# Block 0 of a fused WKV and feed-forward kernel: weight words made by two VectorE operations, low bits by ScalarE, gate transposes a slice later

## The chip, the cores and the metric

The kernel runs on one core of a Trainium2 chip. The metric is the device time of one execution in microseconds (us). The engines of the core are TensorE (PE in the rows, its weight loads PEld), VectorE (DVE), ScalarE (ACT), GpSimd (POOL) and SyncE (SP), which issues most of the transfers. Each engine works through its own list of instructions in order; semaphores tie the lists together.

## The reference

Three stages work on 3072 tokens (4 sequences of 768) of 384 channels. The gated feed-forward stage has a hidden width of 1536, and its weights reach the kernel as float64 words; the third stage sends each token to the one of 8 experts with the largest logit.

```
for t in range(S):                                   # attention, per batch and head of 48
    y[:, :, t] = einsum(r_t, state + u * k_t v_t)
    state = w * state + k_t v_t
g = x @ w_gate                                       # feed-forward, 384 -> 1536 -> 384
x = (silu(g) * (x @ w_val)) @ w_out
logits = x @ w_gate2                                 # routing, 8 experts
e = argmax(logits); gate_w = softmax(logits)[e]; eom = sigmoid(x @ w_output_gate)[e]
out = gate_w * eom * (max(x @ w1[e], 0) @ w2[e])
```

## The kernel before

The tokens go in 8 blocks of three tiles of 128 tokens. For each block the feed-forward stage (`b_block`) runs over 12 groups f of 128 hidden columns, and between its steps stand the attention of the block's successor, in pieces, and other small work. The order is written out by hand: each block has a list `slots` of 24 entries, and step f of `b_block` issues, in this order, the g product (`b_up`, nine matmuls into bank 3 or 4), `slots[2f]`, the down product of group f-2 (`b_down`), the v product, the activation (`b_act`: silu on ScalarE, product s on VectorE, the cast h on ScalarE and its rest on GpSimd or, after block 0, on VectorE) and `slots[2f+1]`. This text calls that a step.

Matmuls take each operand as a rounded part (hi) and a rest (lo), three products for one. So each weight group W{f} has a hi and a lo half, and in block 0 they have to be made. For each f a load on SP's queue brings 128 x 2304 int32 words to a tile `raw` (the float64 words, low and high half in turn). `conv_steps` makes float32 bits of them in a tile `cv`: in three chunks of 384 words, three VectorE operations for each (lines 214 to 216), with bank 5 between them. This text calls the whole conv(f). `conv_b` casts cv to the hi half (ScalarE, line 232) and subtracts for the lo half (GpSimd, line 233). `gate_a` turns the third chunk of cv with three TensorE transposes (line 241) into bank 7 and copies it out as `gt` (ScalarE, line 243); `gate_b` multiplies `gt` by the small matrix G (line 249), and three small copies put the result in the last 16 columns of W{f} (lines 252 to 254). The group f can be used by `b_up` once W{f} is there, and by `b_down` once `gate_b` is through.

Bank 7 is shared: by `gate_a` and `gate_b`, by the attention's scores (`a_scores`, line 363, every second matmul) and by its state product (line 427). So whoever writes it waits until the one before has been read.

Before block 0 the program prepares tables and the attention of the first three tiles, and conv(0) and conv(1) are done. In block 0 conv(f) stands behind the activation of step f-3, `conv_b(f)` behind that of step f-2. The attention tiles 3, 4 and 5 stand in slots 0 to 22 (`a_place`: scale, diagonal, scores, output, state). In blocks 2 to 5 `scan_units` loads the weights a second time, squares them on GpSimd (line 265) and takes a minimum on VectorE (line 268); `find_flag` looks at the results near the end.

Of the kernel before, what the change touches and what calls it, by code (L numbers as in the profile page):

```python
# [8 lines left out]
F32 = mybir.dt.float32  # L9
F32R = mybir.dt.float32r  # L10
BF16 = mybir.dt.bfloat16
I32 = mybir.dt.int32
U32 = mybir.dt.uint32
I64 = mybir.dt.int64
AF = mybir.ActivationFunctionType
ALU = mybir.AluOpType
AX = mybir.AxisListType
# [34 lines left out]
def kernel(  # L52
# [30 lines left out]
    tid = cst.tile([P, NT], I32, name="tid")  # L83
    cnt = cst.tile([P, 8], F32, name="cnt")
    pw = cst.tile([P, 2, 4, 8], F32, name="pw")
    bad = cst.tile([P, 2 + NF], F32, name="bad")
    badb = cst.tile([P, 1], BF16, name="badb")
    flag = cst.tile([P, 1], I32, name="flag")
    wT = cst.tile([P, 4], F32, name="wT")
# [28 lines left out]
    def setup_consts():  # L118
        dve.memset(wT, 1.0)
        dve.memset(rev, 0.0)  # L120
        act.activation(out=rev, in_=rev, func=AF.Silu)
        dve.memset(kr3[0], 0.0)
        pool.memset(kr3[1], 0.0)
        for j in range(2):
            sp.dma_start(
                out=wT[64 * j : 64 * j + HD, :],
                in_=w_d.rearrange("(p j) d -> j d p", j=2)[j],
            )
        sp.dma_start(out=ub, in_=u_d.rearrange("h d -> (h d)").partition_broadcast(P))
        make_identity(nc, ident)  # L130
        pool.memset(triu, 1.0)
        pool.affine_select(
            out=triu, in_=triu, compare_op=ALU.is_gt, fill=0.0, base=0,
            pattern=[[1, P]], channel_multiplier=-1,
        )
# [63 lines left out]

    cvs = {}  # L200

    def conv_steps(f):
        raw = raws.pop(f)
        r32 = raw.rearrange("p (n two) -> p n two", two=2)
        lo, hi = r32[:, :, 0], r32[:, :, 1]
        if f % 2 == 0:
            t = cpool.tile([P, FW], I32, tag="rows", name="cv", bufs=1)
        else:
            t = apool.tile([P, FW], I32, tag="cv", name="cv", bufs=1)
        cvs[f] = t.bitcast(F32)  # L210
        p = bank[5][:, 0:DM].bitcast(I32)

        def part(o):
            dve.tensor_scalar(p, hi[:, o], 3, 0x3FFFFFF8, ALU.logical_shift_left, ALU.bitwise_and)  # L214
            dve.scalar_tensor_tensor(p, hi[:, o], -0x40000000, p, ALU.bitwise_and, ALU.bitwise_or)  # L215
            dve.scalar_tensor_tensor(t[:, o], lo[:, o], 29, p, ALU.logical_shift_right, ALU.bitwise_or)  # L216

        return [lambda c=c: part(slice(c * DM, (c + 1) * DM)) for c in range(3)]

    def conv_a(f):  # L220
        for u in conv_steps(f):
# [34 lines left out]
    def scan_units(f):  # L256
        st = {}

        def u0():
            st["raw"] = load_w(f)  # L260

        def u1():
            st["t"] = apool.tile([P, FW], F32, tag="cv", name="sc", bufs=1)
            h = st["raw"].bitcast(F32).rearrange("p (n two) -> p n two", two=2)[:, :, 1]
            pool.tensor_tensor(out=st["t"], in0=h, in1=h, op=ALU.mult)

        def u2():
            dve.tensor_reduce(out=bad[:, 2 + f : 3 + f], in_=st["t"], op=ALU.min, axis=AX.X)

        return [u0, u1, u2]  # L270

    def find_flag():
        few = cpool.tile([P, 1], F32, tag="few", name="few", bufs=1)
        dve.tensor_reduce(out=few, in_=cnt, op=ALU.max, axis=AX.X)
        dve.tensor_scalar(bad[:, 1:2], few, float(CAP), None, ALU.is_gt)
        dve.tensor_scalar(few, few, float(CAPS[0]), None, ALU.is_gt)
        dve.tensor_scalar(bad[:, 2:], bad[:, 2:], TINY * TINY, None, ALU.is_lt)
        dve.tensor_reduce(out=badb, in_=bad, op=ALU.max, axis=AX.X)
        return few

# [332 lines left out]
    def a_place(slots, i, first):  # L613
        e = 1 if i % BT == BT - 1 else 0
        if i + 1 < NT:
            slots[first].append(lambda: a_load(i + 1))
        if i < 2 * BT:
            slots[first + (i == BT)].append(lambda: a_scale(i))
            slots[first + 1].append(lambda: a_diag(i, BT < i))
            slots[first + 3 - e] += [lambda: a_keys(i), lambda: a_scores(i), lambda: a_mask(i)]  # L620
            slots[first + 5 - e] += [lambda: a_out(i), lambda: a_load_kr(i + 1), lambda: a_bonus(i + 1)]
            slots[first + 6].append(lambda: a_state_up(i, 7))
            return
        e = 0
        if i == 2 * BT:
            slots[first] += [lambda: a_scale(i), lambda: a_diag(i, False)]
            slots[first + 2] += [lambda: a_scores(i), lambda: a_next(i), lambda: a_load_kr(i + 1)]
        slots[first + 3 - e].append(lambda: a_keys(i))
        if i + 1 < NT:
            slots[first + 3 - e].append(lambda: a_bonus(i + 1))  # L630
            slots[first + 4 - e].append(lambda: a_scale(i + 1))
        slots[first + 5 - e].append(lambda: a_burst(i))
        if i + 1 < NT:
            slots[first + 5 - e].append(lambda: a_diag(i + 1, False))
            slots[first + 6 - e].append(lambda: a_next(i + 1))
        if i + 2 < NT:
            slots[first + 6 - e].append(lambda: a_load_kr(i + 2))
# [165 lines left out]
    with tc.manual_schedule():  # L803
# [49 lines left out]
        a_load_kr(3)  # L853
        next_w(3)
        next_w(4)
        conv_a(1)
        next_w(5)
        a_bonus(3)
# [2 lines left out]
        for blk in range(NBLK):  # L861
# [6 lines left out]
                for t in range(BT):  # L868
                    a_place(slots, (blk + 1) * BT + t, 8 * t)
            if blk == 0:  # L870
                slots[0][0:0] = [lambda: gate_b(0), lambda: conv_b(1, (GV, OUT)), lambda: gate_a(1), lambda: conv_a(2), lambda: a_state(0, 0)]
                slots[1][0:0] = [lambda: gate_b(1), lambda: conv_b(2), lambda: a_state(1, 1)]
                slots[2][0:0] = [lambda: gate_a(2), lambda: a_state(2, 2), lambda: gate_b(2)]
                for f in range(3, NF):
                    slots[2 * f - 5] += [lambda f=f: conv_a(f), lambda f=f: next_w(f + 2) if f > 3 else None]
                    slots[2 * f - 3].insert(0, lambda f=f: conv_b(f)); slots[2 * f - 3 + (f == 3)].insert(0, lambda f=f: gate_a(f))
                    slots[2 * f - 2].insert(0, lambda f=f: gate_b(f)) if f > 3 else slots[4].append(lambda: gate_b(3))
                slots[19].append(lambda: zts.append(late_consts()))
            else:
                for o, u in zip((4, 7, 7) if blk == NBLK - 1 else (12, 15, 15), c_units(blk - 1)):  # L880
                    slots[o].append(u)
# [286 lines left out]
```

## Time and profile before

| | |
|---|---|
| runs | 859.89, 862.46, 864.29 us; median 862.46 |
| the profiled execution | 861.56 us, of which 859.8 us from the first instruction to the last |
| mean granted TensorE clock | 0.985 |
| busy, share of the span | PE 821.9 us (96%), PEld 792.9, DVE 459.8 (53%), ACT 271.2 (32%), POOL 267.9 (31%) |
| chain that ended last, by engine | PE 84%, DVE 8%, DMA 2%, issue 2%, ACT 1% |
| block 0, roughly 34 to 125 us | the lines 214, 215 and 216 make 2% each of that chain |

TensorE is busy nearly throughout, so the time is moved by what makes it wait, by what it has to do, and by its clock. VectorE is the busiest engine only in the first seventh of the span, where it makes the weight words. The granted clock was half (0.50) in three stretches near 21, 42 to 55 and 117 to 123 us of the span and full nearly everywhere else.

### The profile page before, as it was taken

What the parts mean: (1) busy time and instruction counts of PE and PEld (TensorE: products, weight loads), DVE (VectorE), ACT (ScalarE), POOL (GpSimd) and SP (SyncE); (2) the same over time, 40 slices, a digit from 0 to 9 for tenths busy, and PEclk for the clock granted to TensorE, in tenths of its full rate; (3) what the DMA queues carried; (4) which work ended last, traced back from release to release, by engine and by line L of the source; (5) the groups of instructions that cost most, each with busy time, mean ns of one, the idle gap of its engine ahead of it and who ended that gap; (6) DMA issues with size and microseconds to landing.
All of it is one profiled execution on the core that took longest, in us unless ns stands there. A gap on an engine that the chain in (4) does not pass through costs nothing.

```text
span 859.8 us, 13873 instructions
## 1 busy us (share of the span) xinstructions
PE 821.9 (96%) x5427; PEld 792.9 (92%) x5427; DVE 459.8 (53%) x945; ACT 271.2 (32%) x590; POOL 267.9 (31%) x241
## 2 busy tenths in 40 slices
PE   2888889999999999999999999999999999999996
PEld 2677789999999999999999999999999999999996
DVE  7898753354465456456455434243565565465541
ACT  2434342221222212212212221223454454444432
POOL 6756546223425335245244112010110210121022
PEclk9879989999999999999999999999999999999999
DMA  8615413853322323333323210410394444444201
GB/s 249 247 59 209 146 67 100 249 141 123 105 94 78 129 78 107 109 102 130 116 102 130 60 47 29 161 51 1 118 368 142 167 142 127 158 133 163 85 26 36
DMA packets 29769, 104.90 MB, mean 122 GB/s; under 512 B 5175, under 2 KB 14193, under 8 KB 26624
## 3 DMA queue, kind: packets, MB, share of 16 engines
q1 hardware_dynamic: 26368, 94.37, 34.0%
q0 software_dynamic: 3328, 9.56, 2.9%
q8 instruction: 45, 0.74, 0.4%
q14 instruction: 28, 0.23, 0.1%
HBM read 85.84 MB, written 16.41 MB: 119 GB/s over the span
## 4 chain that ended last, share of the span: by engine, by line
PE 84%; DVE 8%; DMA 2%; issue 2%; ACT 1%; SPq 1%; POOL 0%; POOLq 0%; DVEq 0%; ACTq 0%
PE bank L494 31%; PE bank L513 17%; PE bank L708 12%; PE bank L725 12%; PE bank L363 3%; PE bank L390 2%; PE bank L376 2%; DVE bank L215 2%; DVE bank L214 2%; DMA spare<-in_rkv_dram 2%; DVE cv L216 2%; PE bank L673 1%; PE bank L739 1%; SPq L415 1%; DVE krT L316 1%
## 5 line engine op out<-in xcount | busy, mean ns | idle before, releaser
L494 PE MATMUL bank<-xT,W 128*128 128x384 f32 x1728 | 331.4, 342 | 1.5 <-DMA xT<-stage 1.3
L494 PEld LDWEIGHTS bank<-xT,W 128*128 128x128 f32 x1728 | 305.1, 189 | 5.8 <-DMA xT<-stage 2.2
L513 PE MATMUL bank<-W,h 128*128 128x400 f32 x864 | 176.0, 348 | 0.0
L513 PEld LDWEIGHTS bank<-W,h 128*128 128x128 f32 x864 | 155.9, 189 | 0.5 <-issue 0.2
L505 ACT CAST h<-s 128x384 fp32r<-128x384 f32 x96 | 49.2, 513 | 328.4 <-DVE s L503 328.4
L503 DVE TENSOR_TENSOR s<-s,bank 128x384 f32<-128x384 f32 x96 | 53.2, 554 | 161.4 <-PE bank L494 148.6
L725 PE MATMUL bank<-hd,wf 128*128 128x416 f32 (+1 forms) x576 | 113.9, 344 | 0.0
L725 PEld LDWEIGHTS bank<-hd,wf 128*128 128x128 f32 x576 | 104.3, 188 | 0.7 <-DVE hd L712 0.2
L747 POOL DMA_INDIRECT out_dram<-yo,ix x32 | 35.0, 1095 | 200.6 <-DVE yo L743 174.0
L343 POOL TENSOR_TENSOR at<-ident,a 128x1024 f32<-128x1024 f32 x19 | 36.1, 1897 | 149.2 <-PE bank L494 118.2
L712 DVE SCALAR_TENSOR_TENSOR hd<-bank,hd 128x416 fp32r<-128x416 f32 (+1 forms) x64 | 36.7, 573 | 77.1 <-ACT hd L711 77.1
L506 DVE TENSOR_TENSOR h<-s,h 128x384 fp32r<-128x384 f32 x84 | 51.8, 616 | 48.7 <-ACT h L505 48.7
L657 DVE TENSOR_TENSOR wf<-raw,wf 128x768 fp32r<-128x768 f32 x64 | 61.1, 955 | 7.0 <-ACT wf L656 1.2
L502 ACT ACTIVATE s<-bank 128x384 f32<-128x384 f32 x96 | 47.2, 492 | 47.4 <-PE bank L494 47.4
L575 POOL DMA_INDIRECT xs<-rows,slot x24 | 23.8, 991 | 112.8 <-DVE slot L573 51.5
L711 ACT ACTIVATE hd<-bank 128x416 fp32r<-128x416 f32 (+1 forms) x64 | 32.3, 505 | 82.3 <-PE bank L708 81.9
L708 PE MATMUL bank<-xd1h,wf 128*128 128x416 f32 x192 | 58.2, 361 | 0.0
L656 ACT CAST wf<-raw 128x768 fp32r<-128x768 f32 x64 | 52.8, 825 | 0.0
L368 DVE COPY_PREDICATED at<-mask,bank 128x512 f32<-128x512 int32 x42 | 28.5, 732 | 38.7 <-POOL at L343 35.3
L708 PE MATMUL bank<-xd0h,wf 128*128 128x416 f32 x144 | 43.8, 362 | 0.0
L708 PEld LDWEIGHTS bank<-xd1h,wf 128*128 128x128 f32 x192 | 36.0, 188 | 0.5
L324 POOL TENSOR_TENSOR rkv<-rkv,ub 128x384 f32<-128x384 f32 x21 | 21.8, 1037 | 46.3 <-DMA rkv<-in_rkv_dram 46.3
(175 smaller groups left out, 946.9 us busy)
## 6 DMA issues: line engine op xcount, KB each, us to landing
raw<-in_w_dram SPq DMA_DIRECT2D x36, 768.0 KB, 4.4
raw<-in_w_dram SPq DMA_DIRECT2D x22, 1152.0 KB, 7.1
rkv<-in_rkv_dram SPq DMA_DIRECT2D x21, 576.0 KB, 5.4
krT<-in_krT_dram SPq DMA_DIRECT2D x42, 192.0 KB, 3.4
xs<-zt SPq DMA_DIRECT2D x32, 197.0 KB, 6.0
xr<-xs SPq DMA_DIRECT2D x6, 591.0 KB, 5.7
spare<-in_w_dram SPq DMA_DIRECT2D x2, 1152.0 KB, 9.4
xT<-stage SPq DMA_DIRECT2D x42, 48.0 KB, 2.1
```

The source lines that it names most:

```text
L343: pool.tensor_tensor(out=af, in0=bc(ident, 1, [P, NH, P]), in1=bc(a, 2, [P, NH, P]), op=ALU.mult)
L494: pe.matmul(ps[i], W[f][:, wl, o : o + P], x[:, xl, c, :], start=(c == 0 and n == 0), stop=(c == KC - 1 and n == 2),)
L502: act.activation(out=s, in_=g, func=AF.Silu)
L503: dve.tensor_tensor(out=s, in0=s, in1=v, op=ALU.mult)
L505: act.copy(out=h[:, 0], in_=s)
L506: (pool if blk == 0 else dve).tensor_tensor(out=h[:, 1], in0=s, in1=h[:, 0].bitcast(F32), op=ALU.subtract)
L513: pe.matmul(bank[t][:, 0 : DM + 16], h[:, hl, t * P : (t + 1) * P], W[f][:, wl, 2 * KC * P :], start=(f == 0 and n == 0), stop=(f == NF - ...
L656: act.copy(out=wf[:, 0], in_=raw[:, f])
L657: dve.tensor_tensor(out=wf[:, 1], in0=raw[:, f], in1=wf[:, 0].bitcast(F32), op=ALU.subtract)
L708: pe.matmul(ps, wf[:, wl, c * P : (c + 1) * P], xd[xl][:, c, 0:n], start=(i == 0), stop=(i == 3 * KC - 1))
L712: dve.scalar_tensor_tensor(h[:, 1, 0:n], ps, 0.0, h[:, 0, 0:n].bitcast(F32), ALU.max, ALU.subtract)
L725: pe.matmul(bank[c][:, 0:n], wf[:, wl, o : o + P], h[:, hl, 0:n], start=(f == 0 and i == 0), stop=(f == NEF - 1 and i == 2),)
```

## The change

The word is made of two operations for each chunk in place of three. The first (line 229 of the changed kernel) takes the high word from SBUF, shifts it by three and joins it with a value `n`, also from SBUF, into bank 5. The second (line 230) joins the high word with 0x3FFFFFFF and keeps those bits of the first. `n` holds the three low bits and is made for all 1152 words of a group by one ScalarE operation (`conv_low`, line 214 of the changed kernel), which reads every eighth byte of the raw words. It lies in a spare tile, or in the place where another weight group will be.

The order of block 0 changes with it. `gate_a(f)` stands in `slots[2f-1]` and `gate_b(f)` in `slots[2f]` for every f; before they stood two slots earlier for most f. `conv_low(f)` stands in `slots[2f-6]`, and ahead of the block for f=0 and 1. The consts that `late_consts` makes move from slot 19 to 22, and the state update of a block's third tile in the first two blocks moves two slots ahead. The weight scan takes a maximum beside the minimum, which adds one VectorE reduction of 128x1152 for each of its 12 groups.

```diff
+    def conv_low(f):
+        b3 = raws[f].bitcast(U8).rearrange("p (n e) -> p n e", e=8)[:, :, 3]
+        t = spare[f] if f in spare else wpool.tile([P, 2 * FG], F32, tag=f"W{f}", name=f"low{f}")
+        lows[f] = t[:, 0:FW].bitcast(I32)
+        act.activation(out=lows[f], in_=b3, func=AF.Identity, bias=nb, scale=1.0 / 32)
...
-        def part(o):
-            dve.tensor_scalar(p, hi[:, o], 3, 0x3FFFFFF8, ALU.logical_shift_left, ALU.bitwise_and)
-            dve.scalar_tensor_tensor(p, hi[:, o], -0x40000000, p, ALU.bitwise_and, ALU.bitwise_or)
-            dve.scalar_tensor_tensor(t[:, o], lo[:, o], 29, p, ALU.logical_shift_right, ALU.bitwise_or)
+        def word(o):
+            dve.scalar_tensor_tensor(p, hi[:, o], 3, n[:, o], ALU.logical_shift_left, ALU.bitwise_or)
+            dve.scalar_tensor_tensor(t[:, o], hi[:, o], 0x3FFFFFFF, p, ALU.bitwise_or, ALU.bitwise_and)
...
         def u2():
-            dve.tensor_reduce(out=bad[:, 2 + f : 3 + f], in_=st["t"], op=ALU.min, axis=AX.X)
+            for o, op in ((2, ALU.min), (2 + NF, ALU.max)):
+                dve.tensor_reduce(out=bad[:, o + f : o + f + 1], in_=st["t"], op=op, axis=AX.X)
...
-            slots[first + 6].append(lambda: a_state_up(i, 7))
+            slots[first + 6 - 2 * e].append(lambda: a_state_up(i, 7))
...
+        conv_low(0)
         a_scores(1, 2)
...
+        conv_low(1)
         conv_a(1)
...
-                slots[0][0:0] = [lambda: gate_b(0), lambda: conv_b(1, (GV, OUT)), lambda: gate_a(1), lambda: conv_a(2), lambda: a_state(0, 0)]
-                slots[1][0:0] = [lambda: gate_b(1), lambda: conv_b(2), lambda: a_state(1, 1)]
-                slots[2][0:0] = [lambda: gate_a(2), lambda: a_state(2, 2), lambda: gate_b(2)]
-                for f in range(3, NF):
-                    slots[2 * f - 5] += [lambda f=f: conv_a(f), lambda f=f: next_w(f + 2) if f > 3 else None]
-                    slots[2 * f - 3].insert(0, lambda f=f: conv_b(f)); slots[2 * f - 3 + (f == 3)].insert(0, lambda f=f: gate_a(f))
-                    slots[2 * f - 2].insert(0, lambda f=f: gate_b(f)) if f > 3 else slots[4].append(lambda: gate_b(3))
-                slots[19].append(lambda: zts.append(late_consts()))
+                slots[0][0:0] = [lambda: conv_low(2), lambda: gate_b(0), lambda: conv_b(1, (GV, OUT)), lambda: conv_a(2), lambda: a_state(0, 0)]
+                slots[1][0:0] = [lambda: gate_a(1), lambda: conv_b(2), lambda: a_state(1, 1)]
+                slots[2][0:0] = [lambda: gate_b(1), lambda: a_state(2, 2)]
+                for f in range(2, NF):
+                    if f > 2:
+                        slots[2 * f - 5] += [lambda f=f: conv_a(f), lambda f=f: next_w(f + 2) if f > 3 else None]
+                        slots[2 * f - 3].insert(0, lambda f=f: conv_b(f))
+                        slots[2 * f - 6].append(lambda f=f: conv_low(f))
+                    slots[2 * f - 1].insert(0, lambda f=f: gate_a(f))
+                    slots[2 * f].insert(0, lambda f=f: gate_b(f))
+                slots[22].append(lambda: zts.append(late_consts()))
```

Left out of the diff are three tiny setup operations for the bias `nb`, a wider tile `bad`, and one more tiny comparison in `find_flag`.

On ScalarE, around the activation of step 1 of block 0 (bank_64 holds g, bank_68 is bank 7, W_416, W_490 and W_566 are the groups 2, 3 and 4), there stood before:

```order
L253 CAST W_416<-wg 128x16
L502 ACTIVATE s<-bank_64 128x384
L505 CAST h<-s 128x384
L232 CAST W_490<-cv 128x1152
L243 COPY gt<-bank_68 128x384
L252 COPY wg<-bank_68 128x16
L253 CAST W_490<-wg 128x16
L502 ACTIVATE s<-bank_64 128x384
L505 CAST h<-s 128x384
L243 COPY gt<-bank_68 128x384
L232 CAST W_566<-cv 128x1152
```

At the same two activations (of steps 1 and 2) there stand now, with W_480 and W_549 for the groups 3 and 4:

```order
L214 ACTIVATE spare_99<-raw,nb 128x1152
L518 ACTIVATE s<-bank_64 128x384
L521 CAST h<-s 128x384
L246 CAST W_480<-cv 128x1152
L257 COPY gt<-bank_68 128x384
L266 COPY wg<-bank_68 128x16
L267 CAST W_413<-wg 128x16
L214 ACTIVATE spare_100<-raw,nb 128x1152
L518 ACTIVATE s<-bank_64 128x384
L521 CAST h<-s 128x384
L246 CAST W_549<-cv 128x1152
L257 COPY gt<-bank_68 128x384
```

The making of the low bits (line 214) stands ahead of the silu, and the copy `gt` now stands behind the cast of the weight group; from step 2 on it stood ahead of it before.

On TensorE, from the v product of step 1 to the next g product (bank_67 and bank_68 take the scores of tile 3 in turn, W_371 and W_376 are group 1, W_416 and W_413 group 2), there stood before, and stands now:

```order
L494 MATMUL bank_65<-xT,W_371 128x384 x9
L363 MATMUL bank_67<-krT 128x128
L363 MATMUL bank_68<-krT 128x128
...
L494 MATMUL bank_64<-xT,W_416 128x384 x9
L241 MATMUL bank_68<-ident,cv 128x128 x3
```

```order
L510 MATMUL bank_65<-xT,W_376 128x384 x9
L255 MATMUL bank_68<-ident,cv 128x128 x3
L379 MATMUL bank_67<-krT 128x128
L379 MATMUL bank_68<-krT 128x128
...
L510 MATMUL bank_64<-xT,W_413 128x384 x9
L263 MATMUL bank_68<-G,gt 128x16 x3
```

The transposes of a gate (line 241, now 255) stand ahead of the scores here, where they stood behind the next g product; the scores share bank 7 with them.

## Rows read from the trace of the kernel before

**Rows 1.** Windows: busy us of each engine in a stretch, PEclk, DMA share, GB/s.

```profile
28.50:119.30 90.80, 76.94 (x541) 68.42 (x537) 78.29 (x146) 36.73 (x90) 57.28 (x49) 0.91 0.41 146
...
116.70:123.50 6.80, 5.93 (x26) 5.68 (x27) 3.42 (x6) 1.41 (x6) 2.29 (x3) 0.50 0.00 0
```

**Rows 2.** Lines by form, 0 to 130 us: busy us, mean ns | idle before.

```profile
L215 DVE SCALAR_TENSOR_TENSOR bank<-raw,bank 128x384 int32<-128x384 int32 x30 | 16.9, 562 | 1.0
...
L232 ACT CAST W<-cv 128x1152 fp32r<-128x1152 f32 x10 | 11.5, 1154 | 0.0
```

**Rows 3.** Timeline, 82.6 to 86.5 us: start us, us, engine, line, tile; VectorE and GpSimd.

```profile
82.75 2.70 POOL L233 TENSOR_TENSOR W<-cv,W 128x1152 fp32r<-128x1152 f32 x1 [0.43 <-ACT W L232]
...
83.51 0.56 DVE L215 SCALAR_TENSOR_TENSOR bank<-raw,bank 128x384 int32<-128x384 int32 x1
...
85.89 0.55 DVE L216 SCALAR_TENSOR_TENSOR cv<-raw,bank 128x384 int32<-128x384 int32 x1
```

**Rows 4.** Timeline of VectorE: the product s of f=1 to 6.

```profile
55.92 0.55 DVE L503 TENSOR_TENSOR s<-s,bank 128x384 f32<-128x384 f32 x1
...
63.17 0.56 DVE L503 TENSOR_TENSOR s<-s,bank 128x384 f32<-128x384 f32 x1 [0.24 <-PE bank L494]
...
73.26 0.55 DVE L503 TENSOR_TENSOR s<-s,bank 128x384 f32<-128x384 f32 x1
...
80.15 0.55 DVE L503 TENSOR_TENSOR s<-s,bank 128x384 f32<-128x384 f32 x1
...
86.36 0.55 DVE L503 TENSOR_TENSOR s<-s,bank 128x384 f32<-128x384 f32 x1
...
95.43 0.55 DVE L503 TENSOR_TENSOR s<-s,bank 128x384 f32<-128x384 f32 x1
```

**Rows 5.** Timeline, 86 to 95 us: the step of f=5.

```profile
86.59 0.52 PE L241 MATMUL bank<-ident,cv 128*128 128x128 f32 x3 [0.79 <-DVE cv L216]
...
86.94 0.51 ACT L505 CAST h<-s 128x384 fp32r<-128x384 f32 x1 [1.23 <-DVE s L503]
...
87.36 0.47 ACT L243 COPY gt<-bank 128x384 f32<-128x384 f32 x1
...
87.60 1.01 POOL L506 TENSOR_TENSOR h<-s,h 128x384 fp32r<-128x384 f32 x1 [1.97 <-ACT h L505]
...
87.89 1.16 PE L363 MATMUL bank<-krT 64*128 64x128 f32 x14 [0.36 <-ACT gt L243]
...
91.23 1.88 PE L513 MATMUL bank<-W,h 128*128 128x400 f32 x9
...
92.95 1.75 PE L494 MATMUL bank<-xT,W 128*128 128x384 f32 x9
```

**Rows 6.** Timeline, 65 to 68 us: GpSimd and VectorE in the step of f=2.

```profile
65.78 2.66 POOL L233 TENSOR_TENSOR W<-cv,W 128x1152 fp32r<-128x1152 f32 x1 [0.37 <-ACT W L232]
...
67.22 0.55 DVE L214 TENSOR_SCALAR bank<-raw 128x384 int32<-128x384 int32 x1
```

**Rows 7.** Timeline, 263 to 268.5 us, and line 316 alone (ns min/median/max).

```profile
263.48 0.56 DVE L503 TENSOR_TENSOR s<-s,bank 128x384 f32<-128x384 f32 x1 [3.07 <-PE bank L494]
...
264.77 2.42 POOL L265 TENSOR_TENSOR sc<-raw 128x1152 f32<-128x1152 f32 x1
...
265.15 3.12 DVE L316 TENSOR_TENSOR krT<-krT,WT 128x1024 f32<-128x1024 f32 x1
...
L316 DVE TENSOR_TENSOR krT<-krT,WT x21: 1211/1218/3124, 47.5 to 515.2; 128x1024 f32<-128x1024 f32 x21
```

**Rows 8.** Tile q of the routing: ns min/median/max.

```profile
L540 DVE SCALAR_TENSOR_TENSOR q<-rows,rev x8: 182/183/184, 175.6 to 611.0; 128x24 f32<-128x24 f32 x8
...
L543 DVE TENSOR_TENSOR q<-oh,rows x8: 182/182/184, 176.2 to 611.6; 128x24 f32<-128x24 bf16 x8
```

**Rows 9.** Line 268, the weight scan: ns min/median/max.

```profile
L268 DVE TENSOR_REDUCE bad<-sc x12: 1344/1346/1348, 237.5 to 483.3; 128x1 f32<-128x1152 f32 x12
```

**Rows 10.** Timeline at 126 us: the gate product of f=10.

```profile
126.57 0.74 PE L249 MATMUL bank<-G,gt 128*128 128x16 f32 x6
```

More of the change, by code (lines that the diff above doesn't have):

```diff
@@ L14 @@
 I64 = mybir.dt.int64
+U8 = mybir.dt.uint8
 AF = mybir.ActivationFunctionType
@@ L85 @@
     pw = cst.tile([P, 2, 4, 8], F32, name="pw")
-    bad = cst.tile([P, 2 + NF], F32, name="bad")
+    bad = cst.tile([P, 2 + 2 * NF], F32, name="bad")
+    nb = cst.tile([P, 1], F32, name="nb")
+    ni = cst.tile([P, 1], I32, name="ni")
     badb = cst.tile([P, 1], BF16, name="badb")
@@ L120, in setup_consts @@
         dve.memset(rev, 0.0)
+        dve.memset(nb, 0.75)
         act.activation(out=rev, in_=rev, func=AF.Silu)
+        act.activation(out=ni, in_=nb, func=AF.Copy)
+        act.activation(out=nb, in_=ni, func=AF.Copy, scale=-31.0 / 64)
         dve.memset(kr3[0], 0.0)
@@ L200 @@
     cvs = {}
+    lows = {}
+    def conv_low(f):
[3 more added lines that the diff above has]
+        act.activation(out=lows[f], in_=b3, func=AF.Identity, bias=nb, scale=1.0 / 32)
     def conv_steps(f):
@@ L204, in conv_steps @@
         r32 = raw.rearrange("p (n two) -> p n two", two=2)
-        lo, hi = r32[:, :, 0], r32[:, :, 1]
+        hi = r32[:, :, 1]
         if f % 2 == 0:
@@ L210, in conv_steps @@
         cvs[f] = t.bitcast(F32)
+        n = lows.pop(f)
         p = bank[5][:, 0:DM].bitcast(I32)
-        def part(o):
-            dve.tensor_scalar(p, hi[:, o], 3, 0x3FFFFFF8, ALU.logical_shift_left, ALU.bitwise_and)
-            dve.scalar_tensor_tensor(p, hi[:, o], -0x40000000, p, ALU.bitwise_and, ALU.bitwise_or)
-            dve.scalar_tensor_tensor(t[:, o], lo[:, o], 29, p, ALU.logical_shift_right, ALU.bitwise_or)
-        return [lambda c=c: part(slice(c * DM, (c + 1) * DM)) for c in range(3)]
+        def word(o):
+            dve.scalar_tensor_tensor(p, hi[:, o], 3, n[:, o], ALU.logical_shift_left, ALU.bitwise_or)
+            dve.scalar_tensor_tensor(t[:, o], hi[:, o], 0x3FFFFFFF, p, ALU.bitwise_or, ALU.bitwise_and)
+        return [lambda c=c: word(slice(c * DM, (c + 1) * DM)) for c in range(3)]
     def conv_a(f):
@@ L276, in find_flag @@
         dve.tensor_scalar(few, few, float(CAPS[0]), None, ALU.is_gt)
-        dve.tensor_scalar(bad[:, 2:], bad[:, 2:], TINY * TINY, None, ALU.is_lt)
+        dve.tensor_scalar(bad[:, 2 : 2 + NF], bad[:, 2 : 2 + NF], TINY * TINY, None, ALU.is_lt)
+        dve.tensor_scalar(bad[:, 2 + NF :], bad[:, 2 + NF :], 4.0, None, ALU.is_ge)
         dve.tensor_reduce(out=badb, in_=bad, op=ALU.max, axis=AX.X)
```

## The prediction

> **What bounds the kernel now.** I read the page first: TensorE is busy 96% of the span, so that a faster VectorE can only give back time in which TensorE waits. That time lies in block 0. From 28.5 to 119.3 us [rows 1], 90.8 us, TensorE is busy 76.9 and VectorE 78.3, the granted clock is 0.91 on the mean: here, and nowhere else, the two are near each other. TensorE stands still for 13.9 us of this stretch, the most that the change could take out of it besides the clock. A second stretch, 6.8 us at a clock of 0.50 [rows 1], follows at 116.7 us.
>
> Second I read the lines by form. Each of the three operations of a chunk takes 0.56 us [rows 2]; in a row they start every 0.59 us (from the one at 83.51 to the fourth after it at 85.89 it is 2.38 us [rows 3]), so that nine take 5.3 us. The timeline of the product s, one per step, gives the length of each step [rows 4]: 7.25 us for f=1, 10.09 (f=2), 6.89 (f=3), 6.21 (f=4), 9.07 (f=5). They differ by what the attention adds: scores in f=1 and 5, output and state in f=2 (and f=6), little in f=3, 4 and 7. In the little ones VectorE has no free time: s waits for the nine operations ahead of it, which end at 86.44, and starts at 86.36 [rows 3, 4] (starts and ends of neighbours overlap by some hundredths).
>
> Third I read the chain of a scores step [rows 5]: transposes at 86.59, the copy gt at 87.36, then at 87.89 the rest of the scores, which waited for gt, then g, the gate product, down at 91.23 and v at 92.95.
>
> **The change, part by part.** The sum is made against the profiled execution, 861.56 us; the median of the runs is 0.9 above it.
>
> *Two operations for three.* Taken alone, 36 operations fewer, three a group: 1.77 us each, 5.3 becomes 3.55. But the first of the two now reads both inputs from SBUF, where lines 214 to 216 have one SBUF and one PSUM input, and those are 0.56 us beside a running GpSimd subtraction of 2.70 us as without [rows 3]. A two-SBUF operation on VectorE is not: line 316 takes 1.22 us mostly, 3.12 at 265.15, when a GpSimd operation over SBUF ran from 264.77 to 267.19 [rows 7]. It ended at 268.27, 1.08 us after that one: it stood still for GpSimd's whole operation. That row is of a TENSOR_TENSOR with 1024 columns; no row has a SCALAR_TENSOR_TENSOR from two large SBUF tiles beside GpSimd. The bounds are thus no wait at all (3.55 us a group) and a wait for the rest of each GpSimd operation that is met, with 384/1024 of 1.08, 0.4 us, after it. I take the second, being the nearest row with the same operands. The Trainium skill, page "SBUF — State Buffer", section "Who interferes with whom", says it of any VectorE instruction with two SBUF inputs: it contends with GpSimd's reads of SBUF for one lock that is held for the whole instruction. The rows of line 316 agree; by the page the value is the second one, too.
>
> A step of f=3 then goes, from the start of s at 0: first operation 0.47 to 1.02, second to 1.6; h's rest on GpSimd from 1.24 to 2.25 (it starts 1.24 after s at 86.36 [rows 4, 5]) holds up the next first one until 2.66. The cast of W (1.15 [rows 2]), which now follows h directly, ends at 2.2, and GpSimd's subtraction (2.66 to 2.70 us [rows 3, 6]) runs from 2.66 to 5.2 and holds up the third first one until 5.6; the last second one ends at 6.2. Before, the nine ended 5.75 us after s (0.47, the least distance of an operation behind s, and 5.3 from the pitch in [rows 3]). So a little step becomes 0.45 us longer, not 1.77 shorter: f=3, 4 and 7, **+1.35 us**. In the output steps f=2 and 6 the conversion starts late, at 67.22, 1.22 us before the end of the subtraction that runs from 65.78 [rows 6], and pays one such wait and parts of two shorter ones: 3.55 + 1.2 is under 5.3, and **-1.0 us** for both is what I put down.
>
> *The gates, a slice later.* On ScalarE, gt now stands behind the cast of W: after h's 0.51 [rows 5] come 1.15 us [rows 2] that came after gt before, so gt ends 2.53 us after s where it ended 1.47 after (87.83 by 86.36 [rows 4, 5]). Queued behind the W cast are gt and the wg copies; who waits for gt is TensorE, with the scores (bank 7), and behind them g, down and v. In f=5 the scores waited for gt already: 2.53, scores to down 3.34 (87.89 to 91.23), down 1.72 (to 92.95), v 1.86 [rows 5] make 9.5 against 9.07: **+0.45**. In f=1 they did not wait for a gate of their own step, since the transposes stood behind the next g product; now they do, and 7.25 becomes 9.5: **+2.25**. At the end of block 0 the gate of f=11, which was done a step earlier, is still owed after the last conversion: transposes 0.52 [rows 5] and product 0.74 [rows 10], 1.04 us with what overlaps, and 0.8 for gt behind the last cast: **+1.85**.
>
> *Low bits on ScalarE.* One more operation of 128x1152 a group. No row has its form (bytes, every eighth one); the nearest is the W cast, also 128x1152, 1.15 us [rows 2], and twice that, 2.3, is the upper bound; I take 1.2. ScalarE is busy 36.7 of 90.8 us [rows 1], and most of them stand where it idles, before a silu. Not so low(4): its tile is where the raw words of group 3 lie, so it waits for conv(3), and silu(1) and with it s(1) queue behind: 1.2 + 0.5 us after a conversion that itself ends 0.8 later than before (the wait of its first operation for a subtraction of 2.66 us less the operations saved), less 0.7 for the state copies that VectorE makes meanwhile ahead of s(1), an estimate: **+1.8** at s(1) against 55.92 [rows 4]. The conversions 0 to 2 before that I cost at nothing: the gain of their six operations is hidden behind the third block of xT, which TensorE's transposes set, and behind the same waits for GpSimd; without that cover they gain 2.8.
>
> *The clock.* The low stretch at 116.7 us costs half its 6.8 us, 3.4, if it goes; TensorE's waits ahead of it change, since the gate and the steps of f=6 and 7 move against each other. I choose **-2.5**, nearer to its going, between -3.4 and a second such stretch, +3.4.
>
> *Costed at nothing:* the twelve maxima, 1.35 us each [rows 9], in blocks where VectorE idles 3.07 us before s [rows 7]; without that cover 16 us. late_consts and the state update move into slots of the same step group, and the setup operations are a few tenths before the first weights are there.
>
> Sum: 1.8 + 2.25 + 0.45 - 1.0 + 1.35 - 2.5 + 1.85 = 4.2 us; 861.56 + 4.2 = 865.8, and with the 0.9 of the median 866.7.
>
> **The rivals.** *Faster: the first operation does not wait for GpSimd.* Nothing but line 316 speaks for the wait, and that is another operation. Then a conversion is 3.55 us, the steps go by TensorE alone: start -2.8, f=1 +2.25 and f=5 +0.45 as before (they go by gt), output steps -1.45 each, little steps 0, clock -3.4, end +1.85: -4.55, so 857.0 us, 857.9 with the median's offset; a little less if the clock also rises sooner in the first stretches, which these rows don't price. It decides from a wait below 1.7 us a group.
>
> *No change: the parts cancel.* The scores' wait for gt in f=1 is partly hidden, since other work of TensorE stands there, and the low bits are away in time: 1.8 and 2.25 go to half, 4.2 becomes 2.2 or less: 861 to 864.
>
> *Slower: the first operation is slow by itself.* If two SBUF sources made this instruction go at half its rate, 384 columns would cost 0.4 us more (0.56 less some 0.16 that 24 columns cost at once [rows 2, 8]), three times a group, in the nine groups that steps wait for 10.8 us: 866.7 + 10.8 = 877. Against it: line 540, with two float32 sources in SBUF, takes 182 ns for 24 columns, line 543 in the ordinary form 182 as well [rows 8]; but 24 columns tell little. The Trainium skill, page "Vector Engine (DVE) Microarchitecture Reference", section "Points that are easy to get wrong", has such a rule for this instruction when its SBUF sources are not bfloat16; by it the time would be that of this rival, and line 540 does not agree with it.
>
> **How the numbers follow.** A measurement of this kernel can tell about 0.5% from no change, 4.3 us: 858.1 to 866.8. Chances: the wait for GpSimd as worked out 0.50, point 866.5, its own range 862 to 871; parts cancel 0.18; no wait 0.26; half rate 0.06. Half of the first case lies below 866.8. So faster 0.26, same 0.42, slower 0.32. The range of 8 in 10 reaches from 856, which leaves some 0.1 of the faster case out, to 872, above which lie the half rate and a second low stretch of the clock.
>
> **What would show it.** Line 229 in the profile after: with mean near 0.56 us the wait is wrong, near 0.9 to 1.5 with a maximum above 2.5 it is right; a minimum near 0.95 is the half rate. The steps between products s tell f=1 (9.5) and f=3 (7.3). The scores of tile 3 should be released by gt, line 257. Line 214 on ScalarE tells the price of the low bits, and silu(1) should follow low(4) and that the last operation of conv(3). What would make the prediction wrong, above all, is a stretch of low clock that comes, goes or changes its length.

## The result and the profile after

The changed kernel takes 870.89 us (median of 870.03 to 872.49), the kernel before 863.38 in the same comparison; the ratio is 1.0091 with a 95% interval of 1.0063 to 1.0118. That is 7.5 us slower, by 0.9% where 0.5% was forecast. The profiled execution took 870.84 us with a span of 869.1, 9.3 more than before.

The products s, one per step, answer to [rows 4] (timeline of VectorE in the changed kernel, f=1 to 6):

```profile
56.12 0.55 DVE L519 TENSOR_TENSOR s<-s,bank 128x384 f32<-128x384 f32 x1
...
67.48 0.55 DVE L519 TENSOR_TENSOR s<-s,bank 128x384 f32<-128x384 f32 x1 [2.14 <-PE bank L510]
...
76.63 0.56 DVE L519 TENSOR_TENSOR s<-s,bank 128x384 f32<-128x384 f32 x1
...
83.83 0.55 DVE L519 TENSOR_TENSOR s<-s,bank 128x384 f32<-128x384 f32 x1
...
90.65 0.56 DVE L519 TENSOR_TENSOR s<-s,bank 128x384 f32<-128x384 f32 x1 [0.51 <-ACT s L518]
...
101.72 0.56 DVE L519 TENSOR_TENSOR s<-s,bank 128x384 f32<-128x384 f32 x1 [1.79 <-PE bank L510]
```

s(1) is where it was (56.12 by 55.92). Step f=1 went from 7.25 to 11.36 us, f=2 from 10.09 to 9.15, f=3 from 6.89 to 7.20, f=4 from 6.21 to 6.82, f=5 from 9.07 to 11.07. By s(11) the changed kernel is 6.45 us behind (144.40 by 137.95); another 1.55 us come in the blocks 2 to 7 and 1.3 us behind the last s.

The lines by form from 0 to 135 us show the new operations (busy us, mean ns):

```profile
L229 DVE SCALAR_TENSOR_TENSOR bank<-raw,spare 128x384 int32<-128x384 int32 x24 | 23.3, 972 | 0.6
L230 DVE SCALAR_TENSOR_TENSOR cv<-raw,bank 128x384 int32<-128x384 int32 x30 | 16.6, 554 | 1.6
L229 DVE SCALAR_TENSOR_TENSOR bank<-spare,low 128x384 int32<-128x384 int32 x6 | 7.2, 1201 | 0.1
...
L229 DVE SCALAR_TENSOR_TENSOR bank<-raw,low 128x384 int32<-128x384 int32 x6 | 4.0, 669 | 1.7 <-ACT low L214 1.6
...
L214 ACT ACTIVATE spare<-raw,nb 128x1152 int32<-128x1152 uint8 x8 | 10.8, 1350 | 7.6 <-DVE cv L230 6.2 <-DMA raw<-in_w_dram 1.5
```

The second operation takes 0.55 us like every one of them before [rows 2]; the first, with two SBUF inputs, takes 0.97 on the mean in 24 cases and 1.2 in the six of the groups 2 and 3. The low bits cost 1.35 us a group.

What TensorE waited for from 28 to 150 us (us in total, times, longest), first in the kernel before:

```profile
PE bank L241 <- DVE S L441: 2.4, 1, 2.4
PE bank L241 <- DVE cv L216: 2.3, 3, 1.0
...
PE bank L249 <- ACT gt L243: 1.2, 3, 0.6
...
PE bank L241 <- DVE at L368: 0.5, 1, 0.5
PE bank L363 <- ACT gt L243: 0.4, 1, 0.4
```

and in the changed one:

```profile
PE bank L379 <- ACT gt L257: 8.8, 2, 6.8
PE bank L263 <- ACT gt L257: 5.1, 6, 1.3
PE bank L443 <- ACT gt L257: 2.0, 2, 1.4
```

The transposes' waits for VectorE fell from 8.5 us, of which three groups are shown, to 2.0, as they now stand two slots later. In their place the readers of gt wait 15.9 us (8.8 + 5.1 + 2.0), where such waits were under 2. The longest, 6.8 us, begins at 51.86 and ends in step f=1, the step that grew most. The timeline of the changed kernel from 47 to 61 us shows what stands behind it, engine by engine:

```profile
47.91 3.18 POOL L247 TENSOR_TENSOR W<-cv,W 128x1152 fp32r<-128x1152 f32 x1 [0.43 <-ACT wg L266]
51.03 2.23 POOL L359 TENSOR_TENSOR at<-ident,a 128x1024 f32<-128x1024 f32 x1
...
46.52 2.04 DVE L332 TENSOR_TENSOR krT<-krT,WT 128x1024 f32<-128x1024 f32 x1
...
48.95 2.56 DVE L229 SCALAR_TENSOR_TENSOR bank<-spare,low 128x384 int32<-128x384 int32 x1
...
52.20 1.48 DVE L229 SCALAR_TENSOR_TENSOR bank<-spare,low 128x384 int32<-128x384 int32 x1
...
54.30 0.57 DVE L229 SCALAR_TENSOR_TENSOR bank<-spare,low 128x384 int32<-128x384 int32 x1
54.90 0.55 DVE L230 SCALAR_TENSOR_TENSOR cv<-spare,bank 128x384 int32<-128x384 int32 x1
...
56.12 0.55 DVE L519 TENSOR_TENSOR s<-s,bank 128x384 f32<-128x384 f32 x1
...
54.30 1.34 ACT L214 ACTIVATE spare<-raw,nb 128x1152 int32<-128x1152 uint8 x1 [6.16 <-DVE cv L230]
...
56.71 0.51 ACT L521 CAST h<-s 128x384 fp32r<-128x384 f32 x1 [0.69 <-DVE s L519]
57.13 1.15 ACT L246 CAST W<-cv 128x1152 fp32r<-128x1152 f32 x1
58.18 0.47 ACT L257 COPY gt<-bank 128x384 f32<-128x384 f32 x1
...
51.07 0.79 PE L379 MATMUL bank<-krT 64*128 64x128 f32 x2
58.70 2.07 PE L379 MATMUL bank<-krT 64*128 64x128 f32 x14 [6.84 <-ACT gt L257]
60.71 2.77 PE L510 MATMUL bank<-xT,W 128*128 128x384 f32 x9
```

The first operation of conv(3) at 48.95 takes 2.56 us. It ends at 51.51, 0.42 us after the GpSimd subtraction (47.91 + 3.18 = 51.09); the next one, at 52.20, ends at 53.68, 0.42 after GpSimd's diagonal at 53.26. This is line 316 of [rows 7] over again, in the other kind of instruction. Beside an idle GpSimd, at 54.30, the same operation takes 0.57. conv(3) lasts 6.5 us in place of 5.4, s(1) follows it, and then h, the W cast and gt follow s(1) on ScalarE one by one. The scores stand idle until gt ends at 58.65.

The windows of the changed kernel (columns as in [rows 1]; the fourth figure from the right is PEclk, the granted clock, before DMA share and GB/s) tell the rest of the step, and of f=5:

```profile
46.00:52.00 6.00, 5.03 (x36) 4.23 (x36) 5.85 (x6) 2.11 (x5) 5.09 (x3) 0.76 0.02 6
52.00:58.50 6.50, 0.00 (x0) 0.00 (x0) 4.49 (x8) 3.50 (x5) 2.90 (x4) 0.50 0.00 0
58.50:60.00 1.50, 1.29 (x12) 1.30 (x13) 0.00 (x0) 0.15 (x1) 1.50 (x1) 0.50 0.00 0
...
63.00:66.00 3.00, 3.00 (x21) 3.00 (x20) 2.23 (x4) 1.83 (x4) 0.22 (x1) 1.00 0.01 3
86.00:93.00 7.00, 4.88 (x29) 4.48 (x29) 4.56 (x6) 6.34 (x16) 4.74 (x5) 1.00 0.62 225
...
94.00:96.50 2.50, 2.50 (x15) 2.28 (x12) 1.77 (x3) 0.00 (x0) 2.48 (x2) 0.50 0.24 96
```

From 52 to 58.5 us TensorE does nothing. When it starts again, it is granted 0.50, which is 1.2 of 2.4 GHz; the full clock is back from 63. The wait did not bring the half clock about: the mean is 0.76 from 46 to 52 us, since the clock fell at 49 us, while TensorE was at work, and it stayed down through the wait. In step f=5 the clock is full up to the wait and half behind it, as the rows at 93 us show:

```profile
93.24 1.87 PE L379 MATMUL bank<-krT 64*128 64x128 f32 x14 [1.95 <-ACT gt L257]
95.03 2.69 PE L510 MATMUL bank<-xT,W 128*128 128x384 f32 x9
```

The g product of that step before:

```profile
88.97 1.84 PE L494 MATMUL bank<-xT,W 128*128 128x384 f32 x9
```

The wait for gt is 1.95 us, and the scores take 1.87 us where they took 1.16, the g product 2.69 where it took 1.84 (the scores' row of before is in [rows 5]). That is 1.56 us of the two that this step grew.

### The profile page after: what moved, and what is told of

Read it like the earlier page. It is cut to its first block, busy times and chain, and to the rows that moved or that the text cites. A ratio compares the mean times of both kernels' runs of the same rounds, so it can differ in the third digit from the quotient of the medians.

```text
span 869.1 us, 13866 instructions
## 1 busy us (share of the span) xinstructions
PE 822.4 (95%) x5427; PEld 793.4 (91%) x5427; DVE 472.3 (54%) x923; ACT 286.1 (33%) x604; POOL 274.0 (32%) x241
## 4 chain that ended last, share of the span: by engine, by line
PE 79%; DVE 8%; issue 5%; ACT 3%; DMA 2%; SPq 1%; POOL 0%; POOLq 0%; DVEq 0%
PE bank L510 31%; PE bank L529 16%; PE bank L724 11%; PE bank L741 11%; PE bank L379 3%; DVE bank L229 3%; PE bank L406 2%; PE bank L392 2%; SPq L431 1%; PE bank L689 1%; DVE krT L332 1%; DVE cv L230 1%; PE bank L755 1%; DVE s L519 1%; ACT W L246 1%
## 5 line engine op out<-in xcount | busy, mean ns | idle before, releaser
L522 DVE TENSOR_TENSOR h<-s,h 128x384 fp32r<-128x384 f32 x84 | 54.0, 642 | 48.6 <-ACT h L521 48.6
```

The lines of the kernel that those rows point to most:

```text
L522: (pool if blk == 0 else dve).tensor_tensor(out=h[:, 1], in0=s, in1=h[:, 0].bitcast(F32), op=ALU.subtract)
```

## The experiments

The chips differ by a little, so each run is told by its ratio to runs of the kernel before on the same chip (95% interval), and its median time. Lengths of steps and waits are from one profile of each kernel. In the edits "..." marks lines left out.

Two theories stood at the start, A and B, as the first expectation puts them.

**The gates back, the rest of the change kept.** The edit gives the old slots, for the groups 1 and 2 too:

```diff
...
-                    slots[2 * f - 1].insert(0, lambda f=f: gate_a(f))
-                    slots[2 * f].insert(0, lambda f=f: gate_b(f))
...
+                    slots[2 * f - 3].insert(0, lambda f=f: conv_b(f)); slots[2 * f - 3 + (f == 3)].insert(0, lambda f=f: gate_a(f))
+                    slots[2 * f - 2].insert(0, lambda f=f: gate_b(f)) if f > 3 else slots[4].append(lambda: gate_b(3))
...
```

> The two-operation words, the low bits and all else of the change, but gate_a and gate_b in the slots of before. Theory A (the time went into TensorE's wait for gt, which the new place of the gates puts behind h and the W cast of the same step): the wait for gt falls from 15.9 us to about 2, the step of f=1 from 11.4 to under 8, and the time to 857 to 863 us. Theory B (the time went into VectorE's first operation, which waits for GpSimd's hold on SBUF): gates make no difference to it, 868 to 872.

1.0015 (1.0002 to 1.0028), 864.61 us: most of the loss is gone, and the waits for gt fell from 15.9 to 3.2 us. A part of theory A failed: the time is above its range, and step f=1 was still 10.97 us. TensorE now waited there for something else:

```profile
51.79 1.16 PE L379 MATMUL bank<-krT 64*128 64x128 f32 x16
55.81 3.25 PE L510 MATMUL bank<-xT,W 128*128 128x384 f32 x9 [2.85 <-ACT s L518]
...
61.56 3.35 PE L529 MATMUL bank<-W,h 128*128 128x400 f32 x9
```

The g product of step 2 waits 2.85 us for silu(1), which follows low(4), which follows the second of the three chunks of conv(3); at the half clock a down product then takes 3.35 us instead of 1.88.

**Three operations at the new place of the gates.** The edit takes `conv_steps` of before and drops every `conv_low`:

```diff
...
-            dve.scalar_tensor_tensor(p, hi[:, o], 3, n[:, o], ALU.logical_shift_left, ALU.bitwise_or)
-            dve.scalar_tensor_tensor(t[:, o], hi[:, o], 0x3FFFFFFF, p, ALU.bitwise_or, ALU.bitwise_and)
+            dve.tensor_scalar(p, hi[:, o], 3, 0x3FFFFFF8, ALU.logical_shift_left, ALU.bitwise_and)
+            dve.scalar_tensor_tensor(p, hi[:, o], -0x40000000, p, ALU.bitwise_and, ALU.bitwise_or)
+            dve.scalar_tensor_tensor(t[:, o], lo[:, o], 29, p, ALU.logical_shift_right, ALU.bitwise_or)
...
```

> The new place of the gates, but words of three operations without low bits on ScalarE, as before the change. Theory A: as slow as the change or slower, 870 to 876, with the step of f=1 above 10 us. Theory B: back to the time before, 861 to 865.

1.0085 (1.0057 to 1.0113), 870.34 us: as slow as the change without any of its words. Theory A holds, theory B as the whole cause falls.

**gt ahead of the W cast.**

```diff
-                        slots[2 * f - 3].insert(0, lambda f=f: conv_b(f))
+                        slots[2 * f - 3].insert(1, lambda f=f: conv_b(f))
```

> The changed kernel with gate_a ahead of conv_b in its slot, so that the copy gt stands ahead of the W cast on ScalarE; nothing else differs. Theory A: gt ends 1.15 us earlier in each step whose scores, state or gate product wait for it, some 6 to 8 of them, so 862 to 866. Theory B: 869 to 872, since the conversions are as long as they were.

1.0079 (1.0059 to 1.0099), 870.52 us: no gain that can be told. A miss of theory A as I had put it. The longest wait for gt was still 6.9 us: there gt is late because it follows s and h, and the 1.15 us of the cast hardly count. Elsewhere the exchange did what theory A says: the steps f=5 and f=9 shortened by 1.05 us each (11.07 to 10.02, 9.31 to 8.26), f=1 by 0.48, and all waits for gt came to 12.3 us in place of 15.9. But s(1) came 0.64 us later, f=2, 6 and 8 grew by 0.40, 0.38 and 0.79, and by s(11) nothing was left of it (144.44 by 144.40). So the cast's place moves the loss more than it makes it.

**The first operation with one SBUF input.**

```diff
-            dve.scalar_tensor_tensor(p, hi[:, o], 3, n[:, o], ALU.logical_shift_left, ALU.bitwise_or)
+            dve.tensor_scalar(p, hi[:, o], 3, -8, ALU.logical_shift_left, ALU.bitwise_and)
```

> The changed kernel, whose first operation leaves n out and so reads one SBUF input (the three low bits of each weight word are left out; ScalarE still makes them). Every operation should take 0.56 us and a conversion 3.55. Theory A: the steps that wait for gt stay as long, 867 to 870.5. Theory B: all of the loss and more comes back, 857 to 862.

1.0015 (1.0001 to 1.003), 863.98 us. Here theory A was wrong, and the range of theory B was not reached: without the wait for GpSimd 0.76% (6.6 us) come back at the new place of the gates as well. Each first operation takes 0.56 us:

```profile
L229 DVE TENSOR_SCALAR bank<-raw 128x384 int32<-128x384 int32 x30 | 16.7, 558 | 0.7
...
L229 DVE TENSOR_SCALAR bank<-spare 128x384 int32<-128x384 int32 x6 | 3.3, 557 | 0.1
...
51.38 0.56 DVE L519 TENSOR_TENSOR s<-s,bank 128x384 f32<-128x384 f32 x1
```

s(1) comes at 51.38, 4.7 us earlier, and that is most of it; the step f=1 itself stays at 11.05 us, with a wait of 2.4 for gt. So both causes are real, and in block 0 they are one chain: conversion, s, h, gt, TensorE.

**low(4) into another spare tile, with the gates back.**

```diff
-        t = spare[f] if f in spare else wpool.tile([P, 2 * FG], F32, tag=f"W{f}", name=f"low{f}")
+        t = spare[6 if f == 4 else f] if f in spare else wpool.tile([P, 2 * FG], F32, tag=f"W{f}", name=f"low{f}")
```

> The gates in the slots of before, and low(4) written to the spare tile 6 instead of 4, so that it no longer waits for conv(3) and silu(1) no longer queues behind that. Theory C (with the gates back, what is left of the loss in the step of f=1, 10.97 us by 7.25, is TensorE's 2.9 us wait for silu(1) and the half clock after it): the step falls to 7.3 to 8.5 us, the time by 2 to 3.5 us against the kernel with the gates back, to 860 to 862.5. Rival (the step is long because conv(3) is): 864 to 865.

1.0018 (1.0001 to 1.0035), 864.31 us, step f=1 10.94 us. Theory C falls. silu(1) was early (52.03), and TensorE waited for the next thing that hangs on s(1):

```profile
53.08 1.85 PE L510 MATMUL bank<-xT,W 128*128 128x384 f32 x9
59.51 0.90 PE L255 MATMUL bank<-ident,cv 128*128 128x128 f32 x3 [4.58 <-DVE at L384]
```

The transposes wait 4.58 us for bank 7, which the mask has to read first, and the mask (line 384) follows s(1), which follows conv(3).

**low(4) into another spare tile, in the changed kernel.** The same edit of `conv_low`, and nothing else.

> The changed kernel with low(4) in the spare tile 6, nothing else. By theory A the scores of the step f=1 wait for gt(2), which follows s(1), and s(1) waits for conv(3), not for silu(1): the step stays above 10.5 us and the time at 869 to 871. If the wait of low(4) were what made that step long, 866 to 868.

1.0093 (1.0073 to 1.0113), 871.05 us, step f=1 11.16 us: as theory A had it. low(4) is not what makes the step long, and it does not hold up s(1) either: step f=0 was 10.80 us with it moved and 10.82 without.

**The gates back, free words, no low bits.** The old slots, the first operation with one SBUF input (the "free words" of this and later headings), and no `conv_low` any more:

```diff
...
-            dve.scalar_tensor_tensor(p, hi[:, o], 3, n[:, o], ALU.logical_shift_left, ALU.bitwise_or)
+            dve.tensor_scalar(p, hi[:, o], 3, -8, ALU.logical_shift_left, ALU.bitwise_and)
...
-        conv_low(0)
...
-        conv_low(1)
...
-                    slots[2 * f - 1].insert(0, lambda f=f: gate_a(f))
...
+                    slots[2 * f - 3].insert(0, lambda f=f: conv_b(f)); slots[2 * f - 3 + (f == 3)].insert(0, lambda f=f: gate_a(f))
...
```

> The gates in the slots of before, words of two operations with one SBUF input each and no low bits at all (the three low bits of each weight word are left out, and ScalarE does not make them). If the two-SBUF operation and the low bits eat the gain of the shorter conversion, this one shows it: s(1) at 51 to 52 us, the steps of f=1 to 8 no longer than before, 855 to 859 in all. If TensorE bounds block 0 anyway, 861 to 863.

0.9861 (0.9834 to 0.9887), 852.2 us: 12 us faster than before, more than I expected. The two-operation conversion is worth that much where its first operation has one SBUF input and no low bits are made.

**Without the maxima.**

```diff
...
-            for o, op in ((2, ALU.min), (2 + NF, ALU.max)):
+            for o, op in ((2, ALU.min),):
...
```

> The changed kernel without the twelve maxima of the weight scan (their place in the check is filled with zeros). If the two small shifts of 1.2 and 0.3 us in blocks 3 and 5 of its profile come from them, 869 to 869.8; if the reductions are hidden and the shifts are transfers that come late by chance, 870.5 to 871.

1.0114 (1.0089 to 1.0139), 872.43 us: not faster. The reductions are hidden, and the shift in block 3 was there again (1.0 us). It does not look like chance: at the first s of block 3 it is 0.6 to 1.2 us in the profiles of all eight kernels with the gates a slice later, and 0.03 at most in the six others. The smaller one in block 5, 0.3 us, is in all nine in which ScalarE makes low bits and in none of the others.

**The gates back, free words, low bits made but not used.**

```diff
...
-            dve.scalar_tensor_tensor(p, hi[:, o], 3, n[:, o], ALU.logical_shift_left, ALU.bitwise_or)
+            dve.tensor_scalar(p, hi[:, o], 3, -8, ALU.logical_shift_left, ALU.bitwise_and)
...
-                    slots[2 * f - 1].insert(0, lambda f=f: gate_a(f))
...
+                    slots[2 * f - 3].insert(0, lambda f=f: conv_b(f)); slots[2 * f - 3 + (f == 3)].insert(0, lambda f=f: gate_a(f))
...
```

> The gates in the slots of before, words of two operations with one SBUF input each (the low bits are left out of the words), but ScalarE still makes them. Against the same kernel without the making of the low bits, 852.2 us, this prices that making: 852 to 853 if ScalarE's idle time hides it, 855 to 858 if low(4), which waits for conv(3) and holds up silu(1), and low(1), which holds up conv(1), reach the end.

0.989 (0.9863 to 0.9916), 853.63 us: between the two expectations, 0.3% above the kernel without them, with intervals that overlap. With the short conversion s(1) stands at 49.83, and step f=1 is 7.52 us. In the kernel without the low bits they were 51.38 and 10.37: there TensorE had the half clock from 54.25 to 61.5 us, here from 40 to 47.25, before that step.

**The new place of the gates, free words, no low bits.**

```diff
...
-            dve.scalar_tensor_tensor(p, hi[:, o], 3, n[:, o], ALU.logical_shift_left, ALU.bitwise_or)
+            dve.tensor_scalar(p, hi[:, o], 3, -8, ALU.logical_shift_left, ALU.bitwise_and)
...
-        conv_low(0)
...
-        conv_low(1)
...
-                        slots[2 * f - 6].append(lambda f=f: conv_low(f))
...
```

> The new place of the gates, words of two operations with one SBUF input each and no low bits at all (they are left out). If the new place costs the same 6 us whatever the conversion takes, 857.5 to 859.5; if it costs only where a conversion holds up the product s that gt follows, 853 to 855.

1.0004 (0.9985 to 1.0024), 863.84 us: above both ranges. The second expectation failed, as the place costs 1.4% even where conversions are short, and the first as well, as that is twice the 6 us it named.

**The wait for GpSimd taken from group 3 alone.** 

```diff
-            dve.scalar_tensor_tensor(p, hi[:, o], 3, n[:, o], ALU.logical_shift_left, ALU.bitwise_or)
+            if f == 3:
+                dve.tensor_scalar(p, hi[:, o], 3, -8, ALU.logical_shift_left, ALU.bitwise_and)
+            else:
+                dve.scalar_tensor_tensor(p, hi[:, o], 3, n[:, o], ALU.logical_shift_left, ALU.bitwise_or)
```

> The changed kernel, with the first operation free of the second SBUF input for the group 3 alone (the low bits of that group are left out). If the wait for GpSimd is paid in conv(3), which stands beside a subtraction of 2.6 and a diagonal of 1.9 us on GpSimd: s(1) at 52 to 53 instead of 56.1 us, and the time at 865 to 867.5. If it is paid a little in each group: 869.5 to 870.5.

1.0061 (1.004 to 1.0083), 868.02 us, a little above the range for conv(3). s(1) came 3.5 us earlier, and by s(11) 3.9 us were left of it (140.53 by 144.40):

```profile
48.35 0.55 DVE L230 TENSOR_SCALAR bank<-spare 128x384 int32<-128x384 int32 x1
49.00 0.56 DVE L233 SCALAR_TENSOR_TENSOR cv<-spare,bank 128x384 int32<-128x384 int32 x1
...
52.59 0.56 DVE L522 TENSOR_TENSOR s<-s,bank 128x384 f32<-128x384 f32 x1
```

At this place of the gates the wait costs 0.76% in all groups together (1.0091 by 1.0015). Some 0.3% of it are paid in this one (1.0091 by 1.0061, intervals that overlap), the rest in the others.

**The rest of the change alone.** To the kernel before, with the setup operations and the comparison in `find_flag` among the lines left out:

```diff
...
-            dve.tensor_reduce(out=bad[:, 2 + f : 3 + f], in_=st["t"], op=ALU.min, axis=AX.X)
+            for o, op in ((2, ALU.min), (2 + NF, ALU.max)):
+                dve.tensor_reduce(out=bad[:, o + f : o + f + 1], in_=st["t"], op=op, axis=AX.X)
...
-            slots[first + 6].append(lambda: a_state_up(i, 7))
+            slots[first + 6 - 2 * e].append(lambda: a_state_up(i, 7))
...
-                slots[19].append(lambda: zts.append(late_consts()))
+                slots[22].append(lambda: zts.append(late_consts()))
```

> The kernel before with only the rest of the change: the twelve maxima, late_consts in slot 22, the state update of the third tile two slots ahead, the setup operations. As costed in the prediction: no difference, 862 to 864. Rival: these cost a part of the loss that the gates, the words and the low bits leave unexplained, 865 to 866.

0.9989 (0.9973 to 1.0006), 862.01 us: no difference, as costed.

Together, as ratios to the kernel before:

| words | gates of before | gates a slice later | the place costs |
|---|---|---|---|
| three operations (the rest of the change with both) | 0.9989 | 1.0085 | 0.96% |
| two, two SBUF inputs, low bits (the change) | 1.0015 | 1.0091 | 0.76% |
| two, one SBUF input, low bits made | 0.9890 | 1.0015 | 1.25% |
| two, one SBUF input, no low bits | 0.9861 | 1.0004 | 1.43% |

Down a column, the second SBUF input costs 1.25% (10.8 us of 862) with the old gates and 0.76% (6.6 us) with the new. The intervals of the ratios are some 0.15 to 0.3% to either side, so that every cost here is clear of noise, but not every difference between two costs.

## Why the prediction came out as it did

**The first operation's wait for GpSimd: right, in mechanism and in size.** The prediction took the upper bound from a TENSOR_TENSOR, with 0.4 us after the GpSimd operation; it is 0.42 us in two rows of the SCALAR_TENSOR_TENSOR, and without it 0.76 to 1.25% come back. The rule of the Trainium skill, page "SBUF — State Buffer", section "Who interferes with whom", agrees with these rows. The little steps f=3, 4 and 7 grew by 0.31, 0.61 and 0.38 us, 1.30 in all by 1.35. At equal gates the whole of words and low bits is 0.26% slower than three operations (1.0015 by 0.9989), and the intervals overlap, so that two operations gained nothing. In the working of the little step a subtraction of 2.66 us from 2.66 would end at 5.3, not 5.2; in the trace it ran from 2.2 to 5.1 us after s(3) (78.86 and 81.76 by 76.63).

**The rival of the half rate: wrong, as it was thought to be.** Where GpSimd is quiet the first operation takes 0.57 us, the pace of one SBUF input. The rule of the Trainium skill, page "Vector Engine (DVE) Microarchitecture Reference", section "Points that are easy to get wrong", does not agree with this, and the measurement decides.

**The start and f=1: the sum right by luck, both terms wrong.** 1.8 at s(1) and 2.25 in f=1 make 4.05; measured were 0.2 and 4.11, 4.31. conv(3) was longer than I had it (6.5 us), but conv(0) to conv(2), which I costed at nothing, gained what it lost (s(0) came 0.9 earlier; they have nine operations fewer, not six). The wait of silu(1) for low(4) cost nothing: low(4) began at 54.30, behind the second chunk and not the third, and the run that moved it left step f=0 as it was. The step f=1 was costed as a chain through gt from s(1). That chain was right, as gt ended 2.53 us after s(1) (58.65 by 56.12), but at the half clock, which was left out, the scores took 2.07 us and g 2.77, 1.84 more than the 1.16 and 1.84 of the full one. The runs show how much the clock does to this step. In four kernels that have 50 to 52 matmul records in it (windows from s(1) to s(2)):

| kernel | step f=1, us | TensorE busy | idle | mean granted clock |
|---|---|---|---|---|
| gates back, free words, low bits made | 7.52 | 6.95 | 0.57 | 1.00 |
| gates later, free words, low bits made | 11.05 | 8.62 | 2.43 | 0.85 |
| the change | 11.36 | 8.78 | 2.58 | 0.71 |
| gates later, free words, no low bits | 13.89 | 11.31 | 2.58 | 0.63 |

The later gates add 1.9 to 2.0 us of idle time; the rest, 1.7 to 4.4 us, goes with the clock.

**f=5: the term that was mis-sized.** +0.45 was put down and 2.0 came. The step said that gt ends 2.53 us after s and the scores follow; gt did end 2.53 us after s (90.65 to 93.18). What failed is the row of durations behind it: 1.16 for the scores and 1.84 for g are those of the full clock, and after a wait of 1.95 us TensorE ran at the half one: the scores took 1.87 and g 2.69.

**Outputs, clock and end.** f=2 and 6 gave back 0.94 and 1.15 by 0.5 each. The low clock near f=8 did not go, it was halved: a stretch from 124 to 127.6 us in place of the one from 116.6 to 123.3, and the step shortened by 1.1 us, not 2.5 (11.22 by 12.34). The end of the block cost 2.05 by 1.85.

**Behind block 0: nothing costed, 2.85 us measured in the profile.** Of 1.55 us, 1.2 come in block 3, where a product waits for transfers of xT that arrive a little later, and 0.3 in block 5; 1.3 stand behind the last s, with one wait in the expert stage:

```profile
PE bank L510 <- DMA xT<-stage: 2.1, 5, 0.6
PE bank L724 <- issue: 1.6, 1, 1.6
```

The wait at line 724 is 1.1 to 2.0 us in the profiles of all eight kernels with the gates a slice later, and in none of the six with the old ones; so is the shift in block 3. The instructions of these stages are the same. What joins them to the gates stays open. It is no small part: the profiles of the change and of the kernel with the gates back differ by 5.1 us (869.1 by 864.0), of which 2.7 have come by s(11) and 2.4 come behind it.

**The rivals.** "No wait" was priced at 857.9 us; the same gates without the wait measured 863.98. Its price failed at the gates: 4.55 us for them in the prediction, and 0.76 to 1.43% (6.6 to 12 us) here, the least with the wait for GpSimd and the most with the short conversions. The gates were the largest term of the sum, but part of the reason given for it failed: exchanging the W cast and gt won 1.05 us in f=5 and in f=9 and lost as much elsewhere. What stays is that gt, which scores, state and gate product all wait for, now follows s and h of the very step they stand in. With the two-SBUF operation s(1) is the knot of f=1: gt in the changed kernel, silu(1) with the gates back, and the mask with low(4) moved as well each end behind conv(3) or a part of it, and freeing one lets the next hold TensorE. The kernel before has the last of these too, but there TensorE had worked at the half clock from 41.6 to 55.2 us, came to the place late and waited 0.5 us (line 241 for `at`, above).

How much of the gates' whole cost is the wait itself and how much the half clock was not separated: no run holds the clock fixed. Nor does a run move one of `gate_a` and `gate_b` alone.

## What to carry to other kernels

Count an operation by where its operands lie, not only by the number of operations: three VectorE operations that read one SBUF tile each took no longer in all than two of which one reads two (0.9989 by 1.0015 with the old gates, 1.0085 by 1.0091 with the new), beside a GpSimd that was busy 57 of 91 us [rows 1]. When an instruction in an ordered list is moved behind another engine's step, look at what the first engine has to wait for at its new place, and price the wait for its length and for a lower clock that may go with it. A version that beats both kernels follows from this: the gates where they were and the word from two one-input operations, 852.2 us, if the three lowest bits of the weight words may go; one that keeps them was not found.

## What was not expected of the hardware

The wait works both ways. GpSimd's subtraction for a whole group took 2.62 to 2.70 us in all ten cases before. In the changed kernel five of ten took that long; the other five, at 47.91, 78.86, 86.13, 113.14 and 120.41 us, took 3.18, 2.90, 3.00, 2.90 and 2.95, and each began while a VectorE operation with two SBUF inputs was running (line 332 from 46.52 to 48.56 for the first, line 229 for the others).

And a wait of TensorE of only 1.95 us (f=5) was followed by a granted clock of 0.50 from 93.5 to 96.7 us, so that it cost nearly twice its length. The same is in the profiles of all eight kernels with the gates a slice later. Yet the length of a wait alone does not decide it: the wait of 2.4 us in the kernel before (line 241 for `S`, above) was followed by the full clock. The same wait in the kernel with the rest of the change alone, 2.36 us, went with the half one from 73.25 to 77 us, and its step f=3 took 7.62 us in place of 6.89. What decides between the two stays open.
